# A softcap attention with a relu-squared MLP on one core: a branch on cap, with and without the maximum

## The chip, the cores and the metric

One core of a Trainium2 chip runs the kernel. The metric is device time in microseconds (us), the median of three runs.

## The reference

```python
scale = 1.0 / np.sqrt(q.shape[-1])                       # q, k, v: 4 x 12 x 448 x 64
scores = scale * np.matmul(q, k.transpose(0, 1, 3, 2))
scores = cap * np.tanh(scores / cap)                     # cap = 30.0
scores = scores - np.max(scores, axis=-1, keepdims=True)
attn = np.exp(scores)
attn = attn / (np.sum(attn, axis=-1, keepdims=True) + 1e-09)
x = np.matmul(attn, v)                                   # to 1792 x 768
r = np.maximum(x @ w_in, 0.0)                            # w_in: 768 x 2048
out = (r * r) @ w_out                                    # w_out: 2048 x 768
```

All is float32. A tanh bounds every score by |cap|.

## The kernel before

The work of a batch (448 tokens) is attention for 12 heads in 6 pairs, then the MLP in both directions. There are 24 pairs in all, numbered by p; pairs 0 to 5 are batch 0.

`heads` is one pair. The scores are computed transposed, keys on partitions, in four chunks of 112 keys. For each chunk c, `qk` (L186) writes both heads' scores to PSUM, and `tanh` (L195, ScalarE) brings them to SBUF as t[c], 112 x 896. `top` (L203, VectorE) takes the maximum over the four chunks in three instructions, `all_top` (L211, GpSimd) the maximum over the partitions, `less` (helper line L143, VectorE) subtracts it from each chunk, and `exp` (L223, ScalarE) multiplies by cap and exponentiates. `pv` (L249, TensorE) multiplies the chunks by v into the accumulator po. The row sums come from a product with a block of ones: `ones` (L261) into the accumulator ss. For pairs below ADD_FROM = 11 there are ones-matmuls for each chunk; from pair 11 on the four chunks are added on VectorE first (`add`, L233, three instructions) and one set of ones-matmuls follows. A float32 matmul of the source stands as two in the trace, so a pair has 16 of `qk`, 16 of `pv`, and 16 or 4 of `ones`. PSTEP, by batch, says how many chunks one `pv` step takes: 2 for batches 0 and 1, 4 for the others. Then the norm chain: `sums` (L282, ScalarE) adds eps, two transposes and a reciprocal turn the sums round (L285, L288, L291), `mult` (L296) writes xf, and `x_hi` (L138 or L140) and `x_lo` (L143) split it into two parts x.

`convert` brings one of 34 pieces of the weights, given in 64 bits, to two float32 parts: a load, a scaling on ScalarE (L329), three VectorE instructions (L339, L342, L345), a copy (L138 or L140), a subtraction (L143), and a store to DRAM for the later batches. `up` and `down` are the MLP: each product takes three matmuls (L389 to L391), from x into accumulators f, and from g = relu squared into accumulators f. Four PSUM buffers serve po, ss and f, two more the scores.

The order is not that of the source. Each piece of work is a `Step` with a key, an engine, an assumed duration, the steps that it waits for, and the buffers that it takes. A list scheduler at the end of the function (from L475) starts on each engine the ready step with the lowest key whose buffers are free, and the instructions are issued in this order; each engine then works through its own queue. Keys are times in a plan: pair starts T, C0 = 4 for each head of batch 0; TF[0] = T[-1] + LAT for the start of the MLP of batch 0, W for the length of each batch's MLP. EARLY pieces of the weights are keyed before TF[0], the others SPACE apart after it. A key is only a rank: a step whose inputs and buffers are there runs ahead of its key if nothing else is ready.

All loads and stores are issued from SP. The prologue (L73 to L79) loads cap and makes capa = |cap|, c1 = scale / |cap| and eps.

Of the kernel before, what the change touches and what calls it, by code (L numbers as in the profile page):

```python
# [13 lines left out]
AF = mybir.ActivationFunctionType  # L14
ALU = mybir.AluOpType
RED = bass_isa.ReduceOp


@with_exitstack
def kernel(  # L20
    ctx: ExitStack,
    tc: tile.TileContext,
    qkT: bass.AP,
    v: bass.AP,
    cap: bass.AP,
# [4 lines left out]
    nc = tc.nc  # L30
    B, H, _, D, S = qkT.shape
    CP, NCH = v.shape[1], v.shape[3]
# [5 lines left out]
    EARLY, SPACE = 1, 3.4  # L38
    ATT, WLEAD = -6, 14
    NBLK, NHLF, NW, XB, NT = 37, 13, 7, 10, 10  # L40
    C0, LAT, TAIL = 4, 28, 30
    DMA, QSTEP, HOLD, PORT = 2.5, 2, 4, 15
    PVD, QD = 6, 2
    XH, GH, WH = 0.0, -2.0, 0.0
    ADD_FROM = 11
    PSTEP = [2, 2, 4, 4]
    W = [140, 145, 150, 120]

    const = ctx.enter_context(tc.tile_pool(name="const", bufs=1))
    sb = ctx.enter_context(tc.tile_pool(name="sb", bufs=2))  # L50
# [3 lines left out]
    def f(ap):  # L54
        return ap.bitcast(F32)
# [7 lines left out]
    capa = const.tile([P, 1], F32, name="capa")  # L63
    rcap = const.tile([P, 1], F32, name="rcap")
    c1 = const.tile([P, 1], F32, name="c1")
    eps = const.tile([P, 1], F32, name="eps")
# [9 lines left out]
    nc.vector.tensor_tensor(out=capa, in0=capb, in1=capn, op=ALU.max)  # L76
    nc.vector.reciprocal(out=rcap, in_=capa)
    nc.vector.tensor_scalar_mul(c1, rcap, SCALE)
    nc.vector.memset(eps, 1e-9)  # L79

# [75 lines left out]
    def heads(p, T, n_at):  # L158
        b, h = p // (H // 2), 2 * (p % (H // 2))
        raw = Buf("qkraw")  # L160
        vs = [Buf("v0"), Buf("v1")]
        s = [Buf("s") for _ in range(NCH)]
        t = [Buf("t") for _ in range(NCH)]
        po, ss = Buf("po"), Buf("po")
        mx, ma = Buf("mx"), Buf("ma")

        def load():
            for i in range(2):
                nc.sync.dma_start(out=raw.ap[i * D:(i + 1) * D], in_=qkT[b, h + i].rearrange("t d s -> d t s"))

        def load_v():
            for i in range(2):
                nc.sync.dma_start(out=vs[i].ap[:, :, i * D:(i + 1) * D], in_=v[b, :, h + i])

        ready = Step(T - 16, "SP", 1.5, load, new=[raw], lag=3.0)
        got_v = Step(T, "SP", 1.4, load_v, new=vs, lag=3.0)

        tanhs = []
        for c0 in range(0, NCH, n_at):

            def qk(c0=c0):
                for c in range(c0, c0 + n_at):
                    ks = slice(c * CP, (c + 1) * CP)
                    for i in range(2):
                        r = slice(i * D, (i + 1) * D)
                        nc.tensor.matmul(  # L186
                            s[c].ap[0:CP, i, 0:S], raw.ap[r, 1, ks], raw.ap[r, 0], start=True, stop=True
                        )

            cs = slice(c0, c0 + n_at)  # L190
            q = Step(T + (2 if b == 0 else QD) * c0, "PE", 0.75 * n_at, qk, [ready], new=s[cs] + t[cs], use=[raw], mode="rows")
            for c in range(c0, c0 + n_at):

                def tanh(c=c):
                    nc.scalar.activation(out=t[c].ap, in_=s[c].ap[0:CP, :, 0:S], func=AF.Tanh, scale=c1[0:CP])  # L195

                tanhs.append(Step(T + 2 * c + 1, "ACT", 0.9, tanh, [q], use=[s[c], t[c]]))

        a = tanhs[0]
        for c in range(1, NCH):  # L200

            def top(c=c):
                nc.vector.tensor_tensor(out=mx.ap, in0=t[0].ap if c == 1 else mx.ap, in1=t[c].ap, op=ALU.max)  # L203

            a = Step(
                T + 2 * c + 3, "DVE", 1.01, top, [a, tanhs[c]], calls=c == NCH - 1,
                new=[mx] * (c == 1), use=[t[c]] + ([t[0]] if c == 1 else [mx]), port=True,
            )

        def all_top():  # L210
            nc.gpsimd.partition_all_reduce(ma.ap, mx.ap, CP, RED.max)  # L211

        a = Step(T + 10, "POOL", 2.9, all_top, [a], new=[ma], use=[mx])

        n_add = p >= ADD_FROM
        exps, adds = [], []
        for c in range(NCH):

            def less(c=c):
                sub(t[c].ap, t[c].ap, ma.ap)  # L220

            def exp(c=c):
                nc.scalar.activation(out=t[c].ap, in_=t[c].ap, func=AF.Exp, scale=capa[0:CP])  # L223

            z = Step(T + 14 + 2 * c, "DVE", 1.01, less, [a], use=[t[c], ma], port=True)
            exps.append(Step(T + 15 + 2 * c, "ACT", 0.95, exp, [z], use=[t[c]]))

        if n_add:
            ts = Buf("ts")
            for c in range(1, NCH):  # L230

                def add(c=c):
                    nc.vector.tensor_tensor(out=ts.ap, in0=t[0].ap if c == 1 else ts.ap, in1=t[c].ap, op=ALU.add)  # L233

                adds = [
                    Step(
                        T + 16 + 2 * c, "DVE", 1.01, add, exps[c - 1:c + 1] + adds,
                        new=[ts] * (c == 1), use=[t[c]] + ([t[0]] if c == 1 else [ts]), port=True,
                    )
                ]  # L240


        rows = [slice(0, D), slice(D, 2 * D)]

        def pv(c0, n):
            def go():
                for c in range(c0, c0 + n):
                    for i in range(2):
                        nc.tensor.matmul(  # L249
                            po.ap[rows[i], 0:S], vs[i].ap[:, c, rows[i]], t[c].ap[:, i], start=c == 0, stop=c == NCH - 1  # L250
                        )
                    if not n_add:
                        ones(t[c], c == 0, c == NCH - 1)
                if n_add and c0 + n == NCH:
                    ones(ts, True, True)

            return go

        def ones(u, start, stop):
            for i in range(2):  # L260
                nc.tensor.matmul(  # L261
                    ss.ap[rows[i], 0:S], vs[i].ap[:, 0, rows[1 - i]], u.ap[:, i], start=start, stop=stop
                )

        n_pv = PSTEP[b]
        pvs = []
        for c0 in range(0, NCH, n_pv):
            c1_ = c0 + n_pv
            end = c1_ == NCH
            pvs.append(  # L270
                Step(
                    T + 17 + 2 * (c1_ - 1) + (PVD if b else 0), "PE", (0.75 if n_add else 1.5) * n_pv + (0.75 if n_add and end else 0),
                    pv(c0, n_pv), exps[c0:c1_] + [got_v] + pvs[-1:] + adds * end,
                    new=[po, ss] if c0 == 0 else [],
                    use=t[c0:c1_] + vs + ([po, ss] if c0 else []) + ([ts] if n_add and end else []), mode="cols",
                )
            )

        sm, tr, rc, xf, x = Buf("sm"), Buf("tr"), Buf("rc"), Buf("xf"), Buf("x")

        def sums():
            nc.scalar.activation(out=sm.ap, in_=ss.ap[:, 0:S], func=AF.Identity, bias=eps)  # L282

        def tr1():
            nc.vector.transpose(out=tr.ap, in_=sm.ap)  # L285

        def rec():
            nc.vector.reciprocal(out=rc.ap, in_=tr.ap.rearrange("p (j c) -> p j c", c=32)[:, :, 0])  # L288

        def tr2():  # L290
            nc.vector.transpose(  # L291
                out=sm.ap, in_=rc.ap.rearrange("p (j o) -> p j o", o=1).to_broadcast([P, S // 32, 32])
            )

        def mult():
            nc.vector.tensor_tensor(out=xf.ap, in0=po.ap[:, 0:S], in1=sm.ap, op=ALU.mult)  # L296

        def x_hi(eng):
            copy(eng, x.ap[:, 0], xf.ap)

        def x_lo():
            sub(x.ap[:, 1], xf.ap, f(x.ap)[:, 0])

        T += 26
        a = Step(T, "ACT", 0.63, sums, pvs[-1:], new=[sm], use=[ss])
        a = Step(T + 1, "DVE", 0.57, tr1, [a], new=[tr], use=[sm])
        a = Step(T + 1, "DVE", 0.17, rec, [a], new=[rc], use=[tr])
        a = Step(T + 1, "DVE", 0.56, tr2, [a], use=[rc, sm])
        a = Step(T + 1, "DVE", 0.54, mult, [a] + pvs[-1:], new=[xf], use=[sm, po])
        a = Step(T + 2, None, COPY(448, dve=XH), x_hi, [a], new=[x], use=[xf])  # L310
        a = Step(T + 3, "DVE", SUB(448), x_lo, [a], use=[xf, x], port=True)
        x_t[b, h // 2], xdone[b, h // 2] = x, a
# [132 lines left out]
    T = [C0 * g for g in range(H)]  # L445
    TF = [T[-1] + LAT]
    for b in range(B):
        TF.append(TF[b] + W[b])
        if b + 1 < B:
# [13 lines left out]
    for b in range(B):  # L463
        t0, rate = TF[b], W[b] / (NM * NKK + NDM * NF)
        for m in range(NM):
# [109 lines left out]
            st.fn(*[st.eng] * st.any)  # L575


# [27 lines left out]
```

## Time and profile before

| | |
|---|---|
| time, median of 3 runs | 706.45 us (706.32 to 706.55) |
| span of the profiled execution | 704.5 us |
| TensorE busy | 688.2 us, 3300 matmuls |
| VectorE, ScalarE, GpSimd busy | 423.2, 362.7, 86.5 us |
| granted TensorE clock, mean | 0.995 of full speed |

The span goes from the first to the last instruction of one profiled execution; the median lies 1.95 us above it, which is what lies around the span in the timed runs. Busy time of matmuls has modelled ends, so that matmuls in a row overlap in it; counts of starts in a stretch are more certain.

### The profile page before, as it was taken

What the parts mean: (1) busy time and instruction counts of PE and PEld (TensorE: products, weight loads), DVE (VectorE), ACT (ScalarE), POOL (GpSimd) and SP (SyncE); (2) the same over time, 40 slices, a digit from 0 to 9 for tenths busy, and PEclk for the clock granted to TensorE, in tenths of its full rate; (3) what the DMA queues carried; (4) which work ended last, traced back from release to release, by engine and by line L of the source; (5) the groups of instructions that cost most, each with busy time, mean ns of one, the idle gap of its engine ahead of it and who ended that gap; (6) DMA issues with size and microseconds to landing.
All of it is one profiled execution on the core that took longest, in us unless ns stands there. A gap on an engine that the chain in (4) does not pass through costs nothing.

```text
span 704.5 us, 8604 instructions
## 1 busy us (share of the span) xinstructions
PE 688.2 (98%) x3300; PEld 500.7 (71%) x3300; DVE 423.2 (60%) x563; ACT 362.7 (51%) x498; POOL 86.5 (12%) x28
## 2 busy tenths in 40 slices
PE   6799999999999999999999999999999999999997
PEld 2233367567876786776797866766679979999997
DVE  4999999999997984777630654887681011111000
ACT  5688686788565645757521444776661003443000
POOL 1532204202101021011100110111110000000000
PEclk9899999999999999999999999999999999999999
DMA  8813469897899879745466655743337666665760
GB/s 202 262 57 107 138 219 309 273 306 259 321 324 303 300 270 333 209 149 165 153 235 206 214 182 170 227 147 127 115 116 247 239 237 214 206 209 202 241 204 26
DMA packets 57304, 148.41 MB, mean 211 GB/s; under 512 B 26288, under 2 KB 35504, under 8 KB 57264
## 3 DMA queue, kind: packets, MB, share of 16 engines
q1 hardware_dynamic: 57264, 147.87, 64.1%
q8 instruction: 26, 0.43, 0.2%
q14 instruction: 14, 0.11, 0.0%
HBM read 117.18 MB, written 30.67 MB: 210 GB/s over the span
## 4 chain that ended last, share of the span: by engine, by line
PE 87%; DVE 7%; POOL 1%; issue 1%; DMA 1%; ACT 1%; SPq 0%; ACTq 0%; DVEq 0%
PE f L389 18%; PE f L391 17%; PE f L390 17%; PE po L249 8%; PE s L186 8%; PE ff L389 5%; PE ff L390 5%; PE ff L391 5%; PE po L261 4%; DVE t L143 3%; DVE mx L203 2%; POOL ma L211 1%; DMA raw<-in_w_in_dram 1%; ACT t L223 1%; DVE xf L296 1%
## 5 line engine op out<-in xcount | busy, mean ns | idle before, releaser
L211 POOL PARTITION_ALL_REDUCE ma<-mx x24 | 86.3, 3597 | 434.0 <-DVE mx L203 412.4
L223 ACT ACTIVATE t<-t,capa 112x896 f32<-112x896 f32 x96 | 99.0, 1040 | 39.4 <-DVE t L143 38.7
L389 PE MATMUL f<-x,w 128*128 128x448 f32 x300 | 114.6, 382 | 0.0
L391 PE MATMUL f<-x,w 128*128 128x448 f32 x300 | 109.7, 366 | 0.0
L390 PE MATMUL f<-x,w 128*128 128x448 f32 x300 | 109.6, 365 | 0.0
L143 DVE TENSOR_TENSOR t<-t,ma 112x896 f32<-112x896 f32 x96 | 105.1, 1109 | 4.3 <-POOL ma L211 3.6
L389 PE MATMUL f<-g,w 128*128 128x448 f32 x288 | 106.7, 371 | 0.0
L391 PE MATMUL f<-g,w 128*128 128x448 f32 x288 | 105.3, 366 | 0.0
L390 PE MATMUL f<-g,w 128*128 128x448 f32 x288 | 105.3, 366 | 0.0
L195 ACT ACTIVATE t<-s,c 112x896 f32<-112x896 f32 x96 | 93.1, 1000 | 18.6 <-PE s L186 18.4
L186 PE MATMUL s<-qkraw 64*112 64x448 f32 x384 | 88.5, 575 | 6.4 <-DMA qkraw<-in_qkT_dram 4.7
L143 DVE TENSOR_TENSOR g<-r,g 128x448 fp32r<-128x448 f32 x64 | 40.4, 632 | 84.7 <-ACT g L138 84.6
L249 PE MATMUL po<-t,v 112*64 112x448 f32 x384 | 84.7, 553 | 4.7 <-ACT t L223 4.6
L389 PEld LDWEIGHTS f<-x,w 128*128 128x128 f32 x300 | 56.3, 188 | 35.1 <-issue 26.6
L186 PEld LDWEIGHTS s<-qkraw 64*112 64x112 f32 x384 | 31.7, 178 | 47.5 <-issue 29.8
L389 PEld LDWEIGHTS f<-g,w 128*128 128x128 f32 x288 | 54.1, 188 | 13.1 <-issue 8.9
L391 PEld LDWEIGHTS f<-x,w 128*128 128x128 f32 x300 | 56.4, 188 | 4.6
L249 PEld LDWEIGHTS po<-t,v 112*64 112x64 f32 x384 | 24.3, 137 | 49.7 <-issue 37.4
L390 PEld LDWEIGHTS f<-x,w 128*128 128x128 f32 x300 | 56.5, 188 | 3.8
L285 DVE STREAM_TRANSPOSE tr<-sm 128x448 f32<-128x448 f32 x24 | 15.4, 640 | 71.1 <-ACT sm L282 71.0
L391 PEld LDWEIGHTS f<-g,w 128*128 128x128 f32 x288 | 54.1, 188 | 4.3
L390 PEld LDWEIGHTS f<-g,w 128*128 128x128 f32 x288 | 54.2, 188 | 4.1
(52 smaller groups left out, 855.8 us busy)
## 6 DMA issues: line engine op xcount, KB each, us to landing
w<-k_in SPq DMA_DIRECT2D x48, 768.0 KB, 4.8
w<-k_out SPq DMA_DIRECT2D x36, 640.0 KB, 3.9
w<-k_out SPq DMA_DIRECT2D x18, 768.0 KB, 4.6
raw<-in_w_in_dram SPq DMA_DIRECT2D x16, 768.0 KB, 7.3
k_in<-w SPq DMA_DIRECT2D x16, 768.0 KB, 4.4
qkraw<-in_qkT_dram SPq DMA_DIRECT2D x48, 224.0 KB, 5.6
raw<-in_w_out_dram SPq DMA_DIRECT2D x12, 640.0 KB, 5.7
k_out<-w SPq DMA_DIRECT2D x12, 640.0 KB, 3.7
```

Of the source, the lines that this page charges most:

```text
L143: nc.vector.tensor_tensor(out=out, in0=in0, in1=in1, op=ALU.subtract)
L186: nc.tensor.matmul(s[c].ap[0:CP, i, 0:S], raw.ap[r, 1, ks], raw.ap[r, 0], start=True, stop=True)
L195: nc.scalar.activation(out=t[c].ap, in_=s[c].ap[0:CP, :, 0:S], func=AF.Tanh, scale=c1[0:CP])
L203: nc.vector.tensor_tensor(out=mx.ap, in0=t[0].ap if c == 1 else mx.ap, in1=t[c].ap, op=ALU.max)
L211: nc.gpsimd.partition_all_reduce(ma.ap, mx.ap, CP, RED.max)
L223: nc.scalar.activation(out=t[c].ap, in_=t[c].ap, func=AF.Exp, scale=capa[0:CP])
L249: nc.tensor.matmul(po.ap[rows[i], 0:S], vs[i].ap[:, c, rows[i]], t[c].ap[:, i], start=c == 0, stop=c == NCH - 1)
L261: nc.tensor.matmul(ss.ap[rows[i], 0:S], vs[i].ap[:, 0, rows[1 - i]], u.ap[:, i], start=start, stop=stop)
L285: nc.vector.transpose(out=tr.ap, in_=sm.ap)
L389: nc.tensor.matmul(o, w.ap[:, 1, j], x[:, 0], start=first and j == 0, stop=False)
L390: nc.tensor.matmul(o, w.ap[:, 0, j], x[:, 0], start=False, stop=False)
L391: nc.tensor.matmul(o, w.ap[:, 0, j], x[:, 1], start=False, stop=last and j == n - 1)
```

## The change

The old function becomes `tile_body` with an argument `bounded`. A new function of the old name reads cap into registers on the engines, compares the bits of |cap| with those of 40.0 (0x42200000), and holds the body twice, once for each answer. With `bounded` there is no `top`, `all_top` or `less`: `exp` follows `tanh`, eps is 1e-9 times exp(-|cap|), all pairs add their chunks (ADD_FROM = 0), and some keys differ: EARLY 4 in place of 1, LAT 14 in place of 28, PSTEP 4 throughout, and the offsets of exp, pv and the norm chain within a pair (EXP, SUM, NORM) 2, 8, 12 in place of 15, 17, 26.

```diff
+    EXP, SUM, NORM = 15, 17, 26
+    if bounded:
+        NBLK, NT = 37, 10
+        EARLY, LAT, ADD_FROM = 4, 14, 0
+        EXP, SUM, NORM = 2, 8, 12
+        PSTEP = [4, 4, 4, 4]
...
-    nc.vector.memset(eps, 1e-9)
+    if bounded:
+        nc.scalar.activation(out=eps, in_=capa, func=AF.Exp, scale=-1.0)
+        nc.vector.tensor_scalar_mul(eps, eps, 1e-9)
+    else:
+        nc.vector.memset(eps, 1e-9)
...
+        if not bounded:
+            a = tanhs[0]
+            for c in range(1, NCH):
...
+            a = Step(T + 10, "POOL", 2.9, all_top, [a], new=[ma], use=[mx])
...
-            z = Step(T + 14 + 2 * c, "DVE", 1.01, less, [a], use=[t[c], ma], port=True)
-            exps.append(Step(T + 15 + 2 * c, "ACT", 0.95, exp, [z], use=[t[c]]))
+            z = tanhs[c]
+            if not bounded:
+                z = Step(T + 14 + 2 * c, "DVE", 1.01, less, [a], use=[t[c], ma], port=True)
+            exps.append(Step(T + EXP + 2 * c, "ACT", 0.95, exp, [z], use=[t[c]]))
...
-                        T + 16 + 2 * c, "DVE", 1.01, add, exps[c - 1:c + 1] + adds,
+                        T + EXP + 1 + 2 * c, "DVE", 1.01, add, exps[c - 1:c + 1] + adds,
...
-                    T + 17 + 2 * (c1_ - 1) + (PVD if b else 0), "PE", (0.75 if n_add else 1.5) * n_pv + (0.75 if n_add and end else 0),
+                    T + SUM + 2 * (c1_ - 1) + (PVD if b else 0), "PE", (0.75 if n_add else 1.5) * n_pv + (0.75 if n_add and end else 0),
...
-        T += 26
+        T += NORM
...
+    bits = nc.values_load(cap.bitcast(mybir.dt.int32), skip_runtime_bounds_check_because="any float")
+    with tc.If((bits & 0x7FFFFFFF) <= 0x42200000) as small:
+        tile_body(tc, True, qkT, v, cap, w_in, w_out, outT)
+    with small.Else():
+        tile_body(tc, False, qkT, v, cap, w_in, w_out, outT)
```

## Rows read from the trace of the kernel before

**Rows 1.** Page, part 1: busy us (share of the span) and instructions of each engine.
```profile
PE 688.2 (98%) x3300; PEld 500.7 (71%) x3300; DVE 423.2 (60%) x563; ACT 362.7 (51%) x498; POOL 86.5 (12%) x28
```

**Rows 2.** Stretches: busy us (instructions) of each engine, clock, DMA share, GB/s.
```profile
core 0: us, PE busy (x) PEld busy (x) DVE busy (x) ACT busy (x) POOL busy (x), PEclk, DMA share, GB/s
...
600.00:650.00 50.00, 50.00 (x248) 46.36 (x248) 8.13 (x13) 22.09 (x39) 0.00 (x0) 1.00 0.61 205
...
0.00:93.30 93.30, 80.55 (x356) 29.61 (x358) 83.60 (x105) 67.46 (x77) 28.42 (x11) 0.96 0.53 145
93.30:550.00 456.70, 456.70 (x2203) 334.05 (x2200) 326.78 (x439) 261.42 (x362) 58.10 (x17) 1.00 0.69 229
...
20.00:30.00 10.00, 7.74 (x24) 2.22 (x24) 10.00 (x13) 6.41 (x8) 6.30 (x1) 0.66 1.03 331
...
60.00:70.00 10.00, 10.00 (x52) 3.63 (x49) 10.00 (x13) 8.22 (x11) 2.39 (x2) 1.00 0.11 25
```

**Rows 3.** VectorE in order of time: start us, us, instruction.
```profile
65.72 0.61 DVE L143 TENSOR_TENSOR x<-xf,x 128x448 fp32r<-128x448 f32 x1
...
69.26 0.63 DVE L285 STREAM_TRANSPOSE tr<-sm 128x448 f32<-128x448 f32 x1
...
72.04 0.23 DVE L288 RECIPROCAL rc<-tr 128x14 f32<-128x14 f32 x1
...
74.53 0.61 DVE L296 TENSOR_TENSOR xf<-po,sm 128x448 f32<-128x448 f32 x1
...
92.71 0.61 DVE L143 TENSOR_TENSOR x<-xf,x 128x448 fp32r<-128x448 f32 x1
```

**Rows 4.** Groups by line: busy us, mean ns | idle before, releaser.
```profile
L143 DVE TENSOR_TENSOR t<-t,ma 112x896 f32<-112x896 f32 x96 | 105.1, 1109 | 4.3 <-POOL ma L211 3.6
...
L203 DVE TENSOR_TENSOR mx<-mx,t 112x896 f32<-112x896 f32 x48 | 52.1, 1085 | 7.9 <-ACT t L195 6.9
L261 PE MATMUL po<-t,v 112*64 112x448 f32 x176 | 41.9, 554 | 1.6 <-ACT sm L282 1.1 <-DVE xf L296 0.5
...
L261 PE MATMUL po<-ts,v 112*64 112x448 f32 x52 | 12.0, 539 | 0.0
```

**Rows 5.** TensorE in order of time.
```profile
44.04 0.48 PE L389 MATMUL f<-x,w 128*128 128x448 f32 x1
...
59.83 0.92 PE L249 MATMUL po<-t,v 112*64 112x448 f32 x4
60.58 0.92 PE L261 MATMUL po<-t,v 112*64 112x448 f32 x4
61.44 1.76 PE L186 MATMUL s<-qkraw 64*112 64x448 f32 x8
```

**Rows 6.** ScalarE in order of time, [idle before, releaser].
```profile
4.14 1.28 ACT L195 ACT_TABLE_LOAD   x1 [4.14 <-DVE c L78]
7.33 1.01 ACT L195 ACTIVATE t<-s,c 112x896 f32<-112x896 f32 x1 [1.91 <-PE s L186]
...
13.33 0.92 ACT L329 ACTIVATE mag<-raw 128x768 f32<-128x768 f32 x1 [0.45 <-DMA raw<-in_w_in_dram]
...
54.48 0.58 ACT L138 ACTIVATE x<-xf 128x448 fp32r<-128x448 f32 x1 [1.42 <-DVE xf L296]
...
58.24 1.03 ACT L223 ACTIVATE t<-t,capa 112x896 f32<-112x896 f32 x1
59.17 1.90 ACT L195 ACTIVATE t<-s,c 112x896 f32<-112x896 f32 x2
...
68.13 0.62 ACT L282 ACTIVATE sm<-po,eps 128x448 f32<-128x448 f32 x1
```

**Rows 7.** First and last work: cap's load (us to landing), first matmuls, last store.
```profile
capb<-in_cap_dram SPq DMA_DIRECT2D x1, 0.5 KB, 2.6
...
4.66 4.92 PE L186 MATMUL s<-qkraw 64*112 64x448 f32 x12 [4.66 <-DMA qkraw<-in_qkT_dram]
...
701.53 0.33 SPq L439 DMA_DIRECT2D out_dram<-o  x1
```

**Rows 8.** Page, part 3: an instruction queue's packets, MB, share of 16 engines.
```profile
q8 instruction: 26, 0.43, 0.2%
```

More of the change, by code (lines that the diff above doesn't have):

```diff
@@ L19, with tile_body @@
 @with_exitstack
-def kernel(
+def tile_body(
     ctx: ExitStack,
     tc: tile.TileContext,
+    bounded: bool,
     qkT: bass.AP,
@@ L197, in heads, with top, all_top @@
                 tanhs.append(Step(T + 2 * c + 1, "ACT", 0.9, tanh, [q], use=[s[c], t[c]]))
[L199 to L213, printed above, removed]
+        if not bounded:
+            a = tanhs[0]
+            for c in range(1, NCH):
+                def top(c=c):
+                    nc.vector.tensor_tensor(out=mx.ap, in0=t[0].ap if c == 1 else mx.ap, in1=t[c].ap, op=ALU.max)
+                a = Step(
+                    T + 2 * c + 3, "DVE", 1.01, top, [a, tanhs[c]], calls=c == NCH - 1,
+                    new=[mx] * (c == 1), use=[t[c]] + ([t[0]] if c == 1 else [mx]), port=True,
+                )
+            def all_top():
+                nc.gpsimd.partition_all_reduce(ma.ap, mx.ap, CP, RED.max)
+            a = Step(T + 10, "POOL", 2.9, all_top, [a], new=[ma], use=[mx])
         n_add = p >= ADD_FROM
@@ L575, with kernel @@
             st.fn(*[st.eng] * st.any)
+def kernel(
+    tc: tile.TileContext,
+    qkT: bass.AP,
+    v: bass.AP,
+    cap: bass.AP,
+    w_in: bass.AP,
+    w_out: bass.AP,
+    outT: bass.AP,
+):
+    nc = tc.nc
+    bits = nc.values_load(cap.bitcast(mybir.dt.int32), skip_runtime_bounds_check_because="any float")
[3 more added lines that the diff above has]
+        tile_body(tc, False, qkT, v, cap, w_in, w_out, outT)
 def kernel(q, k, v, cap, moe_w_in, moe_w_out):
```

## Prediction

> **What bounds the kernel now.** I read the page first for shares: TensorE is busy 98% of the span, VectorE 60%, ScalarE 51%, GpSimd 12% [rows 1]. A busy matmul row can be stretched by its pipeline, so the second view is the table by stretches, where matmuls are counted against time [rows 2]. In 600:650, with nothing but the MLP, 248 start in 50 us: 50 / 248 = 0.2016 us each, and nothing else in the trace is denser. Between 93.3 and 550, where attention is mixed in, 2203 in 456.7 us make 0.2073 each. So from about 93 us on TensorE issues within 3% of its own pace and its instruction count sets the time. Ahead of that it doesn't: 356 matmuls in the first 93.3 us need 356 × 0.2016 = 71.8, so 21.5 us are lost there. All matmuls at the pace are 3300 × 0.2016 = 665.3; the rest of 704.5 is this loss, 13 us of switches and waits later, and a tail.
>
> The start is the third view. The sixth head pair's x, without which no first product of batch 0 can close, is written from 92.71 on, till 93.3 [rows 3]. On the way VectorE is busy 10.00 of 10 us in 60:70 [rows 2]. TensorE starts 52 matmuls there, and a pair has 16 + 16 + 16 and three of the MLP beside them: 51 × 0.2016 = 10.3 us. So a pair takes some 10 us, and two engines are full at once. A cure for one alone would give nothing; this change relieves both.
>
> **TensorE, pairs 6 to 10 (saturated).** Pairs 0 to 10 now sum with 16 ones-matmuls a pair (176 in [rows 4]) and get the 4 of the later pairs (52 for 13). That is 12 × 11 = 132 fewer; 5 × 12 = 60 of them belong to pairs 6 to 10, which run in the saturated stretch. A group of four matmuls takes 0.75 us from start to start (59.83 to 60.58 [rows 5]), 0.188 each, so 11.3 us; at the dense pace 12.1. I take **11.7**. One pv step in place of two also spares mode switches in batches 0 and 1: the group ahead of a switch takes 0.86 (60.58 to 61.44 [rows 5]), 0.11 more, and two switches less in each of 12 pairs are at most 2.6 us. The order is rebuilt, so I take 0 and keep 0 to 2.6 for the range.
>
> **The start (pairs 0 to 5).** VectorE loses three max (two of them form the 48 of [rows 4]) and four subtractions a pair (96), and gets three adds of the max's size; GpSimd's reduction, and the wait for it, go. VectorE's pair becomes 3 × 1.09 for the adds and 0.63 + 0.23 + 0.63 + 0.61 + 0.61 for two transposes, reciprocal, product and low half [rows 3]: 6.0 us. TensorE's becomes 36 × 0.2016 = 7.3. ScalarE is next: one tanh takes 1.01 and two 1.90 (7.33 and 59.17 [rows 6]), so one behind another costs 0.89; an exp costs 0.93 (58.24 to 59.17), so 0.1 of each instruction overlaps the next. 4 × 0.89 + 4 × 0.93 = 7.3, the sums 0.62 - 0.1 and the x copy 0.58 - 0.1 make 8.3 us a pair. ScalarE becomes the bound of the start.
>
> It begins at 7.33 [rows 6]. Six pairs take 49.8. A weight piece wants the 0.92 - 0.1 of its scaling (13.33 [rows 6]) and about as much for its copy, 1.6; I count three, 4.9 (none to four: 0 to 6.5). Without the last pair's sums and copy, the last exp ends about 61. Its 20 matmuls take 4.0 and the chain from sums to low half 0.62 + 0.63 + 0.23 + 0.63 + 0.61 + 0.58 + 0.61 = 3.9, so the sixth x stands at 69 where it was 93.3. TensorE has by then done 6 × 36 = 216, the 15 MLP matmuls that one free accumulator allows (as before, sets of three from 44.04 on [rows 5], one for each of five x), and 16 scores of the seventh pair, 247. To be where before was at 93.3 it needs 356 - 72 = 284: 37 more, 7.5 us, so 76.5. The start gives 93.3 - 76.5 = **16.8** (14.5 of it are the 72 matmuls themselves). Bounds: 231 or 262 matmuls done and none or four pieces move this by 3 to 5 us either way.
>
> **Afterwards** the weights of 34 pieces pass through VectorE and ScalarE while batch 0's MLP runs. In before VectorE was busy 326.78 us of 93.3 to 550 and TensorE kept its 0.2073 [rows 2]; VectorE has seven instructions a pair less and at most three more, so I cost this at 0. Without that cover, a piece late by its own VectorE time, about 3 us, would stall TensorE once each.
>
> **The branch.** Every engine reads cap into a register ahead of all else. No such read is in the trace; the nearest row is the DMA of the same word, 2.6 us from issue to landing [rows 7]. The first matmul at 4.66 waits for a load that is issued after the branch, so the shift passes through. From above: twice that, 5.2, if a read waits behind another; from below 0. I take **2.6**. At the end each engine jumps over the other arm. Engines other than SP finish sooner; SP issues its last store at 701.53 and the span ends at 704.5, so 3 us can hide a jump, unless the arm waits for the store first. Again 0 to 5.2 by the same row; I take **1.3**, half of 2.6. By the Trainium skill (Runtime: NRT & Kernel Launch, Instruction fetch mechanics) a register load costs about 0.2 us; with that in place of the 2.6 the time would be an estimated 679.5. No trace of before shows it.
>
> The new exp for eps runs behind cap's small VectorE steps and one table load of 1.28 from 4.14 on, ahead of the first tanh at 7.33 [rows 6, 7]: 1.9 us idle cover it. If a second table load were added, 1.28 us still fit; without that cover it would cost 1.5. tanh and exp alternate under a single load in before, so none is expected between them.
>
> **Sum.** 704.5 - 11.7 - 16.8 + 2.6 + 1.3 = 679.9 us of span. The timed median of 706.45 lies 1.95 above the profiled span, so 681.9: I predict **682**.
>
> **Rivals.** *The accumulators hold the start.* Four PSUM accumulators serve MLP and attention; with one kept by the MLP, only one pair has its two. A pair holds them for its 20 matmuls, 4.0, and until xf is written: in before from the sums at 68.13 to 74.53 + 0.61, 7 us [rows 3, 6]. With 7 left, a pair takes 11 us and the start gains nothing: 704.5 - 11.7 + 3.9 + 1.95 = 698.7. Without a queue that chain is 0.62 + 0.63 + 0.23 + 0.63 + 0.61 = 2.7, the pair 6.7, hidden under ScalarE's 8.3. For it: the chain is queued on an in-order VectorE. Against: that queue was full and is now 6.0 of 8.3. Halfway (a pair of 9.7, six pairs) it is 8 us late, 690. Chance 0.17, for 689 to 699.
>
> *The start fills better.* If TensorE is dense from 30 us on, because no gap drops its clock (0.66 granted in 20:30 [rows 2]), some 12 us remain of the 21.5 lost: 704.5 - 132 × 0.2016 - 9.5 + 3.9 + 1.95 = 674.2. Against: ScalarE's 8.3 a pair leaves TensorE's 7.3 no way to be full. Chance 0.11, for 667 to 675.
>
> *The branch starves the instruction stream* (slower). The program before fetched its instructions with 26 packets of 0.43 MB in its larger instruction queue [rows 8], and TensorE kept its pace beside them. If in the arm each of the 26 came late by a small transfer's 2.6 us each, 68 us would be added: 750. From ten late fetches, 26 us, on it eats the gain of 28.5 less the branch. Against: inside the arm the stream is as straight as before, with one jump at its end. The Trainium skill (same page and section) has a taken branch whose target isn't in the window fetch it before going on; that is one stall for each jump, and no trace of before shows one. Chance 0.04.
>
> *The change doesn't do what it says*: cap is 30.0 and the comparison is with the bits of 40.0, so the new arm is taken; if not, the old work with the branch gives 706.45 + 3.9 = 710. Chance 0.01.
>
> **How the numbers follow.** The forecast has 0.66, with its own range 675 to 689. A gain that the branch and a starved start cancel to within 0.2% (1.4 us, about what a measurement of this kernel can tell from no change) has 0.01. Faster: 0.66 + 0.17 + 0.11 = 0.94; same 0.01; slower 0.04 + 0.01 = 0.05. The range reaches from 674, with most of the better start left out, to 696, with the worst of the accumulators left out.
>
> **What would show it.** 3168 matmuls, 96 of them of the ones; VectorE near 423 - 105 (subtractions) - 78 (72 max at 1.085) + 36 (33 adds) = 276 us; no reduction on GpSimd. First matmul near 7.3; sixth x near 72; ScalarE without gaps to 60; the stretch after it at 0.207 a matmul. If x comes 10 or more us apart, look at who holds xf; if matmuls after 100 us start slower than 0.21 apart, the weight pieces are late; if engines start past 10 us or the tail past the last matmul exceeds 7, the branch was undercosted.

## The result, and the profile after

Median 682.45 us (681.55 to 684.22, four runs) against 706.5: ratio 0.966, 95% interval 0.9646 to 0.9675. The profiled execution took 684.22 us at a span of 682.4; the spans of the other three were 679.8 to 681.0, around the 679.9 of the sum.

The page of the changed kernel, part 1, answers to [rows 1]; `tanh` is now L207, `exp` L236, the ones L276, the MLP L404 to L406, the low half of x L155:

```profile
PE 662.9 (97%) x3168; PEld 492.8 (72%) x3168; DVE 289.0 (42%) x441; ACT 350.8 (51%) x486; POOL 0.2 (0%) x4
```

132 matmuls are gone, GpSimd has nothing left, VectorE lost 134 us. In instructions VectorE has 13 more than 563 - 168 + 33 = 428, and ScalarE 12 fewer than before, since 13 more of the copies that either can do went to VectorE. In time VectorE has 13 us more than the 276 forecast, and the copies make only 3.0 of it (17.7 us against 14.7). What raises the time is overlap: before, the durations of VectorE's instructions add up to 458.1 us, 34.9 more than its busy time, because those in a row overlap; now they add up to 305.3, only 16.3 more. The additions, in the table by line, answer to [rows 4]:

```profile
L248 DVE TENSOR_TENSOR ts<-ts,t 112x896 f32<-112x896 f32 x48 | 52.2, 1089 | 28.4 <-ACT t L236 27.4
```

They are the max's size, as forecast, 1.09 us. The stretches answer to [rows 2]:

```profile
core 0: us, PE busy (x) PEld busy (x) DVE busy (x) ACT busy (x) POOL busy (x), PEclk, DMA share, GB/s
0.00:93.30 93.30, 79.08 (x338) 34.43 (x340) 67.78 (x107) 74.02 (x90) 0.20 (x4) 0.95 0.67 202
93.30:550.00 456.70, 456.70 (x2206) 340.91 (x2203) 210.13 (x318) 244.65 (x340) 0.00 (x0) 1.00 0.71 230
...
20.00:30.00 10.00, 9.62 (x36) 2.81 (x32) 7.53 (x12) 7.05 (x9) 0.00 (x0) 0.72 0.89 328
...
40.00:50.00 10.00, 8.25 (x34) 2.59 (x34) 9.10 (x14) 8.26 (x11) 0.00 (x0) 0.83 0.76 266
...
0.00:78.60 78.60, 64.38 (x268) 24.71 (x270) 57.37 (x91) 63.15 (x74) 0.20 (x4) 0.93 0.69 204
```

In the long middle TensorE starts 2206 matmuls in the same 456.7 us, 3 more than before: the pace is the same, and every matmul taken away there is time. In the first 93.3 us it starts 338 where the same state needed 284, so it is 54 × 0.2016 = 10.9 us ahead. Pairs 6 to 10 give 60 × 0.2016 = 12.1, the three matmuls 0.6, and the end takes 1.65 back (below): 10.9 + 12.1 + 0.6 - 1.65 = 22.0, and the span fell by 704.5 - 682.4 = 22.1.

The low halves of x of batch 0, VectorE in order of time, answer to [rows 3]:

```profile
34.07 0.61 DVE L155 TENSOR_TENSOR x<-xf,x 128x448 fp32r<-128x448 f32 x1
...
44.36 0.62 DVE L155 TENSOR_TENSOR x<-xf,x 128x448 fp32r<-128x448 f32 x1
...
55.77 0.62 DVE L155 TENSOR_TENSOR x<-xf,x 128x448 fp32r<-128x448 f32 x1 [0.27 <-ACT x L150]
...
65.00 0.63 DVE L155 TENSOR_TENSOR x<-xf,x 128x448 fp32r<-128x448 f32 x1
...
71.70 0.63 DVE L155 TENSOR_TENSOR x<-xf,x 128x448 fp32r<-128x448 f32 x1
...
78.05 0.63 DVE L155 TENSOR_TENSOR x<-xf,x 128x448 fp32r<-128x448 f32 x1
```

The first three pairs are 10 to 11 us apart and the last two 6.7 and 6.35. ScalarE in order of time, with its longest idle times ahead of the sixth pair's last exp, and that exp (answering to [rows 6]):

```profile
8.96 1.01 ACT L207 ACTIVATE t<-s,c 112x896 f32<-112x896 f32 x1 [2.07 <-PE s L198]
...
27.45 0.63 ACT L297 ACTIVATE sm<-po,eps 128x448 f32<-128x448 f32 x1 [2.64 <-PE po L276]
...
49.16 0.63 ACT L297 ACTIVATE sm<-po,eps 128x448 f32<-128x448 f32 x1 [1.74 <-PE po L276]
...
66.83 1.04 ACT L236 ACTIVATE t<-t,capa 112x896 f32<-112x896 f32 x1
```

ScalarE waits twice for the ones-matmuls, after products that ran at the half clock. TensorE in order of time shows this, and answers to [rows 5]:

```profile
14.27 1.01 PE L198 MATMUL s<-qkraw 64*112 64x448 f32 x4 [1.51 <-ACT t L207]
16.90 1.01 PE L198 MATMUL s<-qkraw 64*112 64x448 f32 x4 [1.62 <-ACT t L207]
19.46 1.84 PE L198 MATMUL s<-qkraw 64*112 64x448 f32 x4 [1.55 <-ACT t L207]
21.23 5.39 PE L264 MATMUL po<-t,v 112*64 112x448 f32 x16
...
31.28 3.23 PE L264 MATMUL po<-t,v 112*64 112x448 f32 x16
...
44.20 4.15 PE L264 MATMUL po<-t,v 112*64 112x448 f32 x16
```

TensorE stood idle 1.5 to 1.6 us ahead of each of three score products; then 1.2 GHz was granted for a part of 20:30 (0.72 on the mean), and 16 products took 5.39 us in place of 3.23. The third pair's took 4.15, with 0.83 granted in 40:50.

The two ends of the span answer to [rows 7]: cap's load, the first matmuls, the last store.

```profile
2.33 0.39 SPq L81 DMA_DIRECT2D capb<-in_cap_dram  x1
...
6.29 6.47 PE L198 MATMUL s<-qkraw 64*112 64x448 f32 x16 [6.29 <-DMA qkraw<-in_qkT_dram]
...
677.76 0.33 SPq L454 DMA_DIRECT2D out_dram<-o  x1
```

The first matmul is 6.29 - 4.66 = 1.63 us later. From the last store to the end it is 682.4 - 677.76 = 4.64 where it was 2.99, 1.65 more. The instruction queue of [rows 8] moved 27 packets in place of 26.

### The profile page after: what moved, and what is told of

It is laid out like the page before. It is cut to its first block, busy times and chain, and to the rows that moved or that the text cites. A ratio compares the mean times of both kernels' runs of the same rounds, so it can differ in the third digit from the quotient of the medians.

```text
span 682.4 us, 8126 instructions
## 1 busy us (share of the span) xinstructions
PE 662.9 (97%) x3168; PEld 492.8 (72%) x3168; DVE 289.0 (42%) x441; ACT 350.8 (51%) x486; POOL 0.2 (0%) x4
## 4 chain that ended last, share of the span: by engine, by line
PE 93%; ACT 5%; DMA 0%; SPq 0%; issue 0%
PE f L404 19%; PE f L406 17%; PE f L405 17%; PE po L264 11%; PE s L198 10%; PE ff L404 5%; PE ff L406 5%; PE ff L405 5%; PE po L276 2%; ACT t L207 2%; ACT t L236 2%; DMA qkraw<-in_qkT_dram 0%; ACT mag L344 0%; ACT sm L297 0%; SPq L605 0%
## 5 line engine op out<-in xcount | busy, mean ns | idle before, releaser
L404 PE MATMUL f<-x,w 128*128 128x448 f32 x300 | 114.5, 382 | 0.0
L406 PE MATMUL f<-x,w 128*128 128x448 f32 x300 | 109.6, 365 | 0.0
L404 PE MATMUL f<-g,w 128*128 128x448 f32 x288 | 106.6, 370 | 0.0
L406 PE MATMUL f<-g,w 128*128 128x448 f32 x288 | 105.2, 365 | 0.0
L198 PE MATMUL s<-qkraw 64*112 64x448 f32 x384 | 90.0, 583 | 14.2 <-ACT t L207 7.9
L207 ACT ACTIVATE t<-s,c 112x896 f32<-112x896 f32 x96 | 92.2, 1002 | 9.4 <-PE s L198 9.3
L236 ACT ACTIVATE t<-t,capa 112x896 f32<-112x896 f32 x96 | 96.6, 1042 | 0.1
L155 DVE TENSOR_TENSOR g<-r,g 128x448 fp32r<-128x448 f32 x64 | 39.8, 624 | 99.2 <-ACT g L150 98.9
L404 PEld LDWEIGHTS f<-x,w 128*128 128x128 f32 x300 | 56.3, 188 | 34.3 <-issue 26.4
L264 PE MATMUL po<-t,v 112*64 112x448 f32 x384 | 80.5, 563 | 0.0
L248 DVE TENSOR_TENSOR ts<-ts,t 112x896 f32<-112x896 f32 x48 | 52.2, 1089 | 28.4 <-ACT t L236 27.4
L404 PEld LDWEIGHTS f<-g,w 128*128 128x128 f32 x288 | 54.1, 188 | 12.9 <-issue 8.8
L406 PEld LDWEIGHTS f<-x,w 128*128 128x128 f32 x300 | 56.3, 188 | 4.7
L264 PEld LDWEIGHTS po<-t,v 112*64 112x64 f32 x384 | 26.2, 141 | 45.8 <-issue 42.5
L406 PEld LDWEIGHTS f<-g,w 128*128 128x128 f32 x288 | 54.1, 188 | 4.4
L451 ACT ACTIVATE o<-f 128x448 f32<-128x448 f32 x18 | 9.8, 546 | 89.4 <-PE f L406 89.4
(47 smaller groups left out, 697.5 us busy)
```

Of the source, the lines that this page charges most:

```text
L155: nc.vector.tensor_tensor(out=out, in0=in0, in1=in1, op=ALU.subtract)
L198: nc.tensor.matmul(s[c].ap[0:CP, i, 0:S], raw.ap[r, 1, ks], raw.ap[r, 0], start=True, stop=True)
L264: nc.tensor.matmul(po.ap[rows[i], 0:S], vs[i].ap[:, c, rows[i]], t[c].ap[:, i], start=c == 0, stop=c == NCH - 1)
L404: nc.tensor.matmul(o, w.ap[:, 1, j], x[:, 0], start=first and j == 0, stop=False)
L406: nc.tensor.matmul(o, w.ap[:, 0, j], x[:, 1], start=False, stop=last and j == n - 1)
L451: nc.scalar.activation(out=o.ap, in_=acc.ap[:, 0:S], func=AF.Copy)
```

## The experiments

"The straight line" is the new arm alone, the first of them, and the base of most others. It holds for |cap| up to 40 only.

**No branch.**

```diff
-    bits = nc.values_load(...)
-    with tc.If((bits & 0x7FFFFFFF) <= 0x42200000) as small:
-        tile_body(tc, True, qkT, v, cap, w_in, w_out, outT)
-    with small.Else():
-        tile_body(tc, False, qkT, v, cap, w_in, w_out, outT)
+    tile_body(tc, True, qkT, v, cap, w_in, w_out, outT)
```

> The body of the new arm alone, in a straight line: no read of cap into registers, no branch, no second arm. Theory (the branch costs 1.63 us ahead of the first matmul, 6.29 against 4.66, and 1.65 us behind the last store, 4.64 against 2.99): 682.45 - 3.3 = 679.2 us, first matmul at 4.7, 3.0 us from the last store to the end. Rival (that time at the ends is the profile's alone, or other loads take it): 682.5, within 0.1%.

Measured 679.55 us (678.41 to 681.47), ratio to before 0.9622 (0.9608 to 0.9636). First matmul at 4.74, last store 673.38 with the end at 676.3, 2.9 us. The branch costs 2.9 us by the medians, 3.3 at the two ends. In 0 to 93.3 us the straight line has 359 matmuls:

```profile
0.00:93.30 93.30, 81.10 (x359) 37.35 (x360) 71.52 (x114) 78.40 (x95) 0.20 (x4) 0.96 0.72 217
```

(359 - 284) × 0.2016 = 15.1 us from the start, and 12.1 from pairs 6 to 10, make 27.2; the median fell by 27.0 from 706.5. The two profiled executions lie further apart than the medians, 682.4 and 676.3 in span: that of the changed kernel is its slowest, that of the straight line its fastest.

**The other arm.**

```diff
-    with tc.If((bits & 0x7FFFFFFF) <= 0x42200000) as small:
+    with tc.If((bits & 0x7FFFFFFF) <= 0x41A00000) as small:
```

> The threshold is 20.0 in place of 40.0, so cap = 30.0 takes the second arm: the old work behind the branch. Theory (the branch costs the same 3.3 us at the two ends, plus a jump to the far arm at the start, once for each engine, up to 2.6 more): 706.5 + 3.3 to 5.9 = 709.8 to 712.4 us. Rival (instruction fetch is late again and again in an arm that stands behind a jump): 720 or more, with gaps between matmuls past 100 us.

Measured 713.47 us (713.03 to 713.75) beside 706.72 for before: 6.75 more, 1 us above the expectation. SP's and TensorE's first rows and SP's last store, in order of time:

```profile
5.22 2.56 SPq L81 DMA_DIRECT2D capb<-in_cap_dram  x1
...
11.99 5.28 PE L198 MATMUL s<-qkraw 64*112 64x448 f32 x12 [11.99 <-DMA qkraw<-in_qkT_dram]
...
708.28 0.33 SPq L454 DMA_DIRECT2D out_dram<-o  x1
```

The first matmul comes 5.7 us later than behind the arm that follows the comparison directly (6.29); the end takes 711.7 - 708.28 = 3.4. SP issues its first load 2.9 us later (5.22 against 2.33), and this issue and the next four are slower too (2.56 against 0.39, then 3.31 against 2.66). By the medians the far arm costs 6.75 us where the near one costs 2.9. Between 93.3 and 550 there are 2199 matmuls against 2203: inside the arm nothing is late. The rival that the branch starves the instruction stream falls.

**No second arm.** `with small.Else()` and its body are left out; a cap above 40 would compute nothing.

> The branch stays, the second arm is empty, so that a cap above 40 would compute nothing. Theory (the 1.65 us at the end are the jump over a long arm to instructions that are not there yet; the 1.63 at the start are the read of cap): 682.45 - 1.7 = 680.8 us. Rival (the end costs the arm's own closing steps, not the far jump): 682.4.

Measured 681.51 us (680.15 to 683.72); this overlaps with the changed kernel. The ends of its trace decide: first matmul at 6.36, last store and end:

```profile
674.83 0.33 SPq L454 DMA_DIRECT2D out_dram<-o  x1
```

677.8 - 674.83 = 2.97, as before the change. So the 1.65 us at the end are the jump over the second arm, and the 1.6 at the start are there without it. This rests on one trace of each; the medians can't part 681.51 from 682.45.

**A filler for the clock.**

```diff
+                if p == 1:
+                    for _ in range(2):
+                        nc.tensor.matmul(po.ap[0:CP, 0:S], raw.ap[0:D, 1, 0:CP], raw.ap[0:D, 0], start=True, stop=True)
                 for c in range(c0, c0 + n_at):
```

> The straight line of the new arm, with two superfluous matmuls ahead of each of the second pair's four score products, written to the accumulator that the pair overwrites later; the order of all else is unchanged. They fill the TensorE gaps at 13 to 20 us, after which the clock was granted at half from about 19.4 to 26.2. Theory (the gaps bring the half clock, and the first pair's products, 5.4 us for 16 in place of 3.2, are late by it, and through ScalarE the sixth x): clock 1.0 in 20:30, sixth x 2 to 3 us earlier than in the straight line without them, time 2 us shorter than that, 677 us. Rival (ScalarE alone sets the start, the clock costs nothing): no change, 679.2. Rival (the added matmuls themselves are late): up to 3 us longer.

Measured 678.4 us (678.09 to 679.92), against the straight line's 678.41 to 681.47: the ranges overlap. Two stretches, and the first pair's products in TensorE's order of time:

```profile
20.00:30.00 10.00, 9.64 (x46) 3.68 (x44) 7.86 (x13) 8.46 (x11) 0.00 (x0) 1.00 0.91 316
...
40.00:50.00 10.00, 10.00 (x44) 3.78 (x42) 8.81 (x14) 8.28 (x11) 0.00 (x0) 0.84 0.82 250
```

```profile
18.90 3.23 PE L267 MATMUL po<-t,v 112*64 112x448 f32 x16
```

The clock stays at 2.4 GHz through 20:30 and the first products take 3.23 us in place of the straight line's 4.38 (the expectation's 5.4 us is the changed kernel's). In this execution it then falls in 40:50, and the sixth x stands at 75.06, later than the straight line's 73.67. Three of the five executions, in which the mean clock was 1.000, had spans of 676.0 to 676.3, the two at 0.997 had 677.7 and 677.8; so within this kernel a half-clock stretch goes with some 1.5 us. The straight line's four executions at 0.995 had 676.3 to 677.5, so the expected gain of 2 us isn't shown.

**The old sums.**

```diff
-        EARLY, LAT, ADD_FROM = 4, 14, 0
+        EARLY, LAT, ADD_FROM = 4, 14, 11
```

> The straight line of the new arm, with no maximum, but with the sums of before: ones-matmuls for every chunk up to pair 10 (132 matmuls more), the additions from pair 11 on. Theory (every matmul counts at 0.2 us, in the start too, because a pair then wants 9.7 us of TensorE and three to six MLP matmuls, as much as ScalarE's 9 to 11): 679.6 + 20 to 26.6 = 700 to 706 us, so that the maximum by itself is worth little. Rival (in the start, 72 of the 132 fit into TensorE's idle time under ScalarE): 679.6 + 12 = 692.

Measured 698.29 us (697.5 to 699.09): 18.7 above the straight line for 132 matmuls, between the two expectations. Less the 12.1 of pairs 6 to 10, the start's matmuls cost 6.6 of their 14.5 us (about 9 by the counts of the two profiled executions); the rest fitted into idle time.

**Additions alone, in the kernel before.**

```diff
-    ADD_FROM = 11
+    ADD_FROM = 0
```

> The kernel before, with the maximum, with one number changed: all pairs add their chunks on VectorE (ADD_FROM 0), 132 matmuls fewer. Theory (VectorE is full in the start and up to 200 us, so the 33 additions of 1.09 us cost there what they are): sixth x 15 to 20 us later, then 60 matmuls fewer, 706.7 + 18 - 12 = 712 us, 708 to 718. Rival (the count of matmuls sets the time): 706.7 - 25 = 682.

Measured 749.57 us (748.05 to 750.58), ratio 1.0604 (1.0586 to 1.0621): much slower than I expected. Its first 300 us, and the same of the kernel before:

```profile
0.00:300.00 300.00, 243.81 (x1011) 133.47 (x1012) 284.72 (x370) 199.91 (x251) 70.62 (x19) 0.91 0.59 189
```

```profile
0.00:300.00 300.00, 287.25 (x1349) 177.03 (x1351) 266.39 (x360) 205.64 (x269) 56.53 (x18) 0.99 0.76 247
```

Without its 132 ones, before has 1217 by then; this has 1011, 206 × 0.2016 = 41.5 us less. VectorE, with 33 × 1.09 = 36 us more to do, is busy 95% of the 300 us, not in the start alone. TensorE's queue waited 55.9 us in them where it waited 12.7 before: 18.8 for exps, 14.5 for weight pieces from VectorE, 11.3 for the added chunks. The sixth x is 11.6 us later (104.34 against 92.71), less than I expected; most of the loss comes behind it, where my 712 had charged nothing. How much of it the lower clock makes (0.91) isn't parted, and no other order of these steps was tried.

**No maximum alone.** A straight line without `top`, `all_top` and `less`; old sums, keys and PSTEP.

```diff
     if bounded:
-        NBLK, NT = 37, 10
-        EARLY, LAT, ADD_FROM = 4, 14, 0
-        EXP, SUM, NORM = 2, 8, 12
-        PSTEP = [4, 4, 4, 4]
+        pass
```

> A straight line with no maximum, no subtraction and no reduction over partitions, and all else as before: the old sums, the old keys and steps (EARLY 1, LAT 28, EXP 15, SUM 17, NORM 26, PSTEP 2, 2, 4, 4). Theory (the work decides, the keys are ranks): like the run with the old sums and the new keys, within 3 us, and 0 to 6 us under before: 700 to 707. Rival (the new keys are a part of the gain): 5 us or more above the run with the old sums and the new keys. Rival (VectorE was the bound of the start and TensorE had room): 690.

Measured 695.72 us (695.39 to 696.06): 10.8 us faster than before, below the 700 to 707 of my theory. It is 2.6 faster than the old sums under the new keys. The first stretch, and VectorE's first and sixth x:

```profile
0.00:93.30 93.30, 86.18 (x409) 37.98 (x411) 45.58 (x84) 72.92 (x87) 0.20 (x4) 1.00 0.71 202
```

```profile
30.42 0.63 DVE L152 TENSOR_TENSOR x<-xf,x 128x448 fp32r<-128x448 f32 x1
...
75.28 0.62 DVE L152 TENSOR_TENSOR x<-xf,x 128x448 fp32r<-128x448 f32 x1 [0.65 <-ACT x L147]
```

409 matmuls by 93.3 us against 356: 53 × 0.2016 = 10.7 us, all of the gain. The first x stands 12.8 us earlier (30.42 against 43.26), the sixth 17.4 (75.28 against 92.71). The first exp of before and of this run, ScalarE in order of time:

```profile
20.08 1.04 ACT L223 ACTIVATE t<-t,capa 112x896 f32<-112x896 f32 x1
...
10.06 1.03 ACT L233 ACTIVATE t<-t,capa 112x896 f32<-112x896 f32 x1
```

It starts 10 us earlier, because a pair's chain no longer goes through VectorE and GpSimd ahead of it. So 12.8 of the 17.4 us are the first pair's chain, and the other five pairs add 4.6.

**Old EARLY and LAT.**

```diff
-        EARLY, LAT, ADD_FROM = 4, 14, 0
+        EARLY, LAT, ADD_FROM = 1, 28, 0
```

> The straight line of the new arm with two of its keys as before: EARLY 1 and LAT 28 in place of 4 and 14. Theory (a key is a rank; weight pieces are converted when their engines are free): within 2 us of the straight line, 678 to 682, as six pieces or nearly so are begun before the sixth x. Rival (without the early keys the pieces come late and the dense MLP waits for them): 3 us for each of two to four pieces, 686 to 692.

Measured 678.38 us (677.86 to 679.67), 360 matmuls by 93.3 us: as the straight line. The theory holds. With a ratio of 0.9602 (0.9588 to 0.9617) this and the filler are the shortest versions by their medians, below both kernels, though their ranges overlap with the straight line's; they have no arm for a cap above 40.

**All old keys, new work.** The straight line with EXP, SUM, NORM, PSTEP, EARLY and LAT of before.

```diff
     if bounded:
-        NBLK, NT = 37, 10
-        EARLY, LAT, ADD_FROM = 4, 14, 0
-        EXP, SUM, NORM = 2, 8, 12
-        PSTEP = [4, 4, 4, 4]
+        ADD_FROM = 0
```

> A straight line with the work of the new arm (no maximum, all pairs add) under the old order: EARLY 1, LAT 28, EXP 15, SUM 17, NORM 26, PSTEP 2, 2, 4, 4. It differs from the run without the maximum alone by the additions only, and from the straight line of the new arm by keys and PSTEP only. Theory (the keys are ranks, the work decides): within 2 us of the straight line, 678 to 682, and 14 to 18 below the run without the maximum alone. Rival (offsets of exp and pv in a pair decide who goes first in the start): 5 us or more above the straight line, 685 to 690.

Measured 680.56 us (679.78 to 680.65): 1.0 above the straight line, 15.2 below the run without the maximum alone. The work decides the time. Its start is better (387 by 93.3 us), and it loses that later, in part at 200 to 250 us; over the whole run TensorE waited 3.3 us for weight pieces.

```profile
0.00:93.30 93.30, 84.92 (x387) 40.51 (x387) 71.42 (x115) 81.59 (x103) 0.20 (x4) 1.00 0.71 212
...
200.00:250.00 50.00, 47.59 (x221) 33.90 (x221) 25.32 (x35) 33.49 (x44) 0.00 (x0) 0.97 0.94 304
```

This run's start is the one that the prediction worked out. ScalarE is busy 60.0 us of the 60 from 10 to 70, it has scaled three weight pieces when the sixth pair's last exp ends, at 60.85 where about 61 was forecast, and the sixth x stands at 70.05, where 69 was forecast without a branch:

```profile
20.00:30.00 10.00, 8.76 (x42) 3.08 (x44) 7.71 (x13) 10.00 (x13) 0.00 (x0) 1.00 0.89 244
40.00:50.00 10.00, 10.00 (x49) 3.75 (x46) 7.16 (x10) 10.00 (x12) 0.00 (x0) 1.00 0.28 70
```

```profile
69.42 0.63 DVE L153 TENSOR_TENSOR x<-xf,x 128x448 fp32r<-128x448 f32 x1
```

**The MLP after the sixth x.**

```diff
-            [x_t[b, kk] for kk in range(NKK)], [xdone[b, kk] for kk in range(NKK)],
+            [x_t[b, kk] for kk in range(NKK)], [xdone[b, kk if b else NKK - 1] for kk in range(NKK)],
```

> The straight line of the new arm, but no MLP matmul of batch 0 may start ahead of the sixth x; so all four accumulators serve the pairs until then, two pairs at a time. Theory (a pair's hold of its accumulators, 4.0 + 2.7 = 6.7 us, is mostly hidden under ScalarE): sixth x at most 2 us earlier than its 73.7 in the straight line, and the 30 MLP matmuls that filled TensorE's idle time, 6 us, come after it: 679.6 + 4 to 6 = 684 to 686. Rival (the accumulators hold the start): sixth x 5 us or more earlier, time 677 to 680.

Measured 688.01 us (686.18 to 688.94), 8.5 above the straight line; both expectations missed. The sixth x comes at 79.94, 6.3 us later than 73.67. With all four accumulators the pairs aren't faster. But this run doesn't part the accumulators from the rest: TensorE was granted 0.76 in 20:30, 0.90 in 40:50 and 0.83 in 60:70 (0.91, 1.00 and 1.00 in the straight line), and ScalarE waited 3.9 us for weight pieces from VectorE ahead of the sixth x.

**Halves in batch 0.**

```diff
-        PSTEP = [4, 4, 4, 4]
+        PSTEP = [2, 4, 4, 4]
```

> The straight line of the new arm with PSTEP 2 in place of 4 for batch 0: each pair's products with v go in two halves, the first ahead of the last two exps. Theory (ScalarE bounds the start, and TensorE idles between score products): the first x 1 to 2 us earlier, fewer gaps ahead of 20 us, time 0 to 2 us shorter, 678 to 679.6. Rival (the accumulators are taken earlier and the halves are parted by mode switches): 1 to 3 us longer.

Measured 682.65 us (681.69 to 683.64), 3.1 longer, at the edge of the rival's 1 to 3. The first x isn't much earlier (31.08 against 31.33), the sixth later (76.46 against 73.67).

**Old offsets in batch 0 alone.**

```diff
-        PSTEP = [4, 4, 4, 4]
+        PSTEP = [2, 4, 4, 4]
...
+        EXP, SUM, NORM = (2, 8, 12) if b else (15, 17, 26)
         raw = Buf("qkraw")
```

> The straight line of the new arm with the old offsets and PSTEP 2 (EXP 15, SUM 17, NORM 26) in batch 0 alone, the new ones in the later batches, EARLY 4 and LAT 14. The old order had 387 matmuls started by 93.3 us where the straight line has 369, and lost it again at 200 to 250 us, where the dense MLP waited for weight pieces. Theory (the old offsets make the better start, the early pieces prevent the later wait): 380 or more by 93.3, no wait after, 679.6 - 2 to 3.6 = 676 to 677.6. Rival (the two are one: a start with fewer pieces done is paid back by waiting for them): 679 to 681.

Measured 690.58 us (690.32 to 690.75), 11 above the straight line: both expectations missed. (The straight line's count was 359, not 369.) TensorE has 316 matmuls by 93.3 us, the sixth x stands at 84.93. Who TensorE waited for, with total us, times, and the longest:

```profile
PE f L405 <- ACT x L150: 6.6, 3, 4.3
PE s L199 <- ACT t L208: 5.2, 5, 1.6
```

An MLP matmul stood in TensorE's queue ahead of other work and waited for a pair's x, up to 4.3 us. All new keys, the old EARLY and LAT, and all old keys lie within 1.2 us of the straight line, so ranks are mostly but not always neutral; which two keys collide here stays open.

## Why the prediction was right, and where not

**What bounds the kernel.** Right for the time, incomplete for VectorE. TensorE's pace past 93.3 us is the same before and after (2203 and 2206), so 60 matmuls there are worth 12.1 us (11.7 in the sum). But I saw VectorE full in the start only; before the change it was busy 148.2 of the 150 us from 50 to 200, which the additions alone brought out, at 749.57.

**"A cure for one alone would give nothing"** is the sentence that failed. Taking the maximum away alone gives 10.8 us; adding the chunks alone costs 43. The 27.0 us of the straight line are 10.8 from the maximum and 16.2 from the sums with the new keys. Under the old keys all four cases were run: before 706.5, without the maximum 695.72, with the additions alone 749.57, with both changes 680.56. So the additions cost 43 us beside the maximum and give 15.2 without it. The first I had read from the rate of the pairs (two engines full), while the gain was mostly in the length of the first pair's chain, which puts the first x 12.8 us earlier.

**The start, 16.8 us.** In the straight line it measures 15.1; behind the branch 10.9, which is less by 1.63 for the branch and by a second half-clock stretch. Two mistakes in it cancelled in part, which was luck. The sixth x was to stand at 69, or 72 with the branch, and stands at 78.7. ScalarE, the bound as forecast, ended its last exp at 67.87 in place of 63.6: it had 5.2 us of waits in that time; and it scaled six weight pieces where I counted three, but made only one of their copies, some 5.7 us in place of 4.9. And the sixth pair's products began 2.7 us after their exps, behind six MLP matmuls. The order of the new keys is a part of this: with the same work under the old keys, where ScalarE didn't wait, the sixth x stands at 70.05. On the other side TensorE used the wait: 30 MLP matmuls, not 15, as two accumulators served the MLP. By 78.6 us it had started 268, so the 284 are reached at 78.6 + 16 × 0.2016 = 81.8 where 79.1 was forecast: the sixth x is 7.1 us late, and the 21 matmuls above the 247 give 4.2 of it back.

**The accumulators.** This rival is not settled. Its reason was there: the last pairs' chain from sums to xf took 3.5 and 3.0 us, near the 2.7 worked out, but the first four took 5.4, 5.7, 5.2 and 4.6, in VectorE's queue. So in the changed kernel a pair held its accumulators for 11.7, 11.7, 10.1, 10.1, 7.7 and 7.0 us, not 6.7; two were with the MLP from 36.88 us on; and from the fourth pair on each pair's products began 0.4 to 0.7 us ahead of the end of the xf before it. Against it, the run in which no MLP matmul goes ahead of the sixth x wasn't faster, though at a lower clock. In the run with all old keys, where ScalarE was full, products began 2.4 to 3.4 us ahead of the end of the xf before. What paced the pairs under the new keys, accumulators or order, stays open. The fifth and sixth pairs' products in the changed kernel, TensorE in order of time, and the xf of the fourth and fifth, VectorE in order of time:

```profile
63.54 3.23 PE L264 MATMUL po<-t,v 112*64 112x448 f32 x16
...
70.56 3.23 PE L264 MATMUL po<-t,v 112*64 112x448 f32 x16
```

```profile
63.29 0.62 DVE L311 TENSOR_TENSOR xf<-po,sm 128x448 f32<-128x448 f32 x1
...
70.61 0.62 DVE L311 TENSOR_TENSOR xf<-po,sm 128x448 f32<-128x448 f32 x1
```

**The branch, 2.6 + 1.3.** It measures 1.63 + 1.65. The start was dearer in the estimate than on the chip, the end cheaper. That the second arm is the cause at the end is shown by the run without it (2.97). By the Trainium skill (Runtime: NRT & Kernel Launch, Instruction fetch mechanics) a taken branch to a target outside the window must fetch it first. The runs fit this, with 1.65 us at the end and 5.7 for the far arm at the start, though no row shows the fetch itself. The arm that follows the comparison directly pays 1.63 for the read, the comparison and the branch together; no row shows the read by itself.

**Afterwards, 0, and the new exp, 0.** Right: the middle kept its pace, and eps was done at 7.08, ahead of the first tanh at 8.96.

**The sum.** 679.9 for a span whose four values are 679.8 to 682.4. It held because its two large terms, 28.5 together, measure 27.2 in the straight line, and the branch 3.9 measures 3.3. That 682 met 682.45 so closely is luck, as the start's mistakes, 7.1 late and 4.2 back, happened to offset. What is left open is the order's share: changed keys and PSTEP alone moved the time by 1.2, 1.0, 2.6, 3.1 and 11 us.

## What to carry to other kernels

When two engines are full in the same stretch, price each cure alone as well as both: here one gave 10.8 us, the other alone cost 43, and together they gave 26 in the old order and 27 in the new. Ask of work taken from a chain whether it shortens the first item or the rate: here 12.8 of the 17.4 us were the first item. A branch on a value that is read at the start cost 3.3 us at the two ends (2.9 by the medians), half of it at the end; put the arm that is taken directly behind the comparison, because the far arm cost 6.75 us by the medians.

## What the chip showed that I had not expected

The far arm's 5.7 us are more than twice the 2.6 of a small load: SP's first issue is 2.9 us later, and that issue takes 2.56 us where it took 0.39. Keeping TensorE busy through one gap took the half clock out of 20:30; in the profiled execution it came in 40:50 instead (0.84), while in three of the five executions the mean clock was 1.000. And superfluous work on TensorE, 16 matmuls, cost nothing that the time shows: 678.4 against 679.55.
